# A written-out instruction order for an attention-plus-MLP kernel: another order for the last groups, four whole-array groups in place of three, and another spread of the last stores

## The chip, the cores and the metric

The kernel runs on one core of a Trainium2 chip. A core has five engines that run side by side, each through its own list of instructions in order: TensorE (PE, matrix products), VectorE (DVE), ScalarE (ACT), GpSimd (POOL) and SyncE (SP, which here issues transfers). They wait for each other through semaphores. Matrix products land in eight banks of accumulator memory, which PE writes and which DVE and ACT can read. Transfers between on-chip memory and device memory (DMA) are issued from the queues of SP, ACT and POOL.

The metric is the device time of one execution in microseconds (us). The profile adds a span: the time from the first to the last instruction of one profiled execution.

## The reference

The reference has two stages. The first is attention with 32 learned "inducing" rows over each of four sequences of 12,480 tokens with 128 channels, done twice (the 32 rows attend to the tokens, then the tokens attend to the result). The second is a two-layer network with 2,048 hidden units and a PReLU on all 49,920 tokens.

```
def mab(q, kv):
    s = scale * (q @ kv.transpose(0, 2, 1))
    a = np.exp(s - s.max(-1, keepdims=True))
    a /= a.sum(-1, keepdims=True) + 1e-09
    return a @ kv
h = mab(I, x)             # 32 x 128 for each sequence
x = mab(x, h)             # 12480 x 128 for each sequence

h = x @ w_in              # 128 -> 2048
g = np.maximum(h, 0.0) + alpha * np.minimum(h, 0.0)
out = g @ w_out           # 2048 -> 128
```

## The kernel before

**The algebra.** The tokens' attention output is a weighted sum of 32 rows, so the kernel never forms it. It multiplies those 32 rows by `w_in` beforehand (`h_weights`, tile `hW`), and the hidden layer then is one product of contraction length 32: the tokens' unnormalised attention weights (tile `rep`, 32 rows, copied four times over the 128 partitions) times `hW`. PReLU is split into a linear part, done by one small matrix (`hA`, function `linear`), and a ReLU part, `relu(h)` times the scaled output weights (`W1`). The attention's denominator is divided out at the very end (`rdT`).

**Groups and chunks.** The 49,920 tokens are cut into 100 groups of up to 512 tokens, 25 for each sequence; the last group of each sequence has 192 tokens. For each group the 2,048 hidden units are 16 chunks of 128. A *fill* (function `fill`) computes one chunk into a bank: a matmul of 32 rows, on one of four row tiles of PE. Then ACT (line 750) or DVE (line 752) empties the bank with a ReLU into a tile `gt`: an *eviction*. In the 192-token groups a fill is two matmuls of 192 columns into one bank, and the eviction is 384 columns wide. A *second* (function `second`) multiplies a chunk's `gt` by `W1` and adds it to the group's own accumulator bank.

**Row tiles.** PE can work as four row tiles of 32 rows each, which run side by side. A second is therefore cut into four matmuls, one for each quarter of the chunk's 128 hidden units. Row tiles must not add to one bank at the same time, so a group goes through row tile 0 for all 16 chunks, then row tile 1, and so on: row tile 3 is the last and works on an older group than row tile 0 does. A second can also be one matmul over the whole array, all 128 rows at once. The constant `WHOLE` (line 25) says how many of the last groups are added up in that way; it was 3, groups 97, 98 and 99.

**The order.** The order of the instructions is written out by hand in the string `PLAN`. Each letter is a step of PE:

- `a` to `h` with a digit: a fill. `a b` are on row tile 0, `c d` on 1, `e f` on 2, `g h` on 3. The first of each pair is emptied by ACT, the second by DVE. The digit is the bank.
- `w x y z`: the next second of row tile 0, 1, 2, 3.
- `v`: the next second over the whole array.
- `l` and `m` with a digit: a group gets its accumulator bank, and the linear part is added (`m` for the groups of `WHOLE`).
- `s` with digits: a pause, in which the products for the attention of a later stretch run.

`pin` ties every instruction to the one recorded before it on the same engine, so the order of the calls is the order on each engine. A fill must wait until its bank has been emptied, a second until its `gt` has been written, and an eviction until its fill is done.

**The end of a group.** After a group's last second, `finish` runs: DVE transposes the accumulator (line 818, `ot`), POOL multiplies by the reciprocal denominators (line 826, `ob`), and four transfers store the result (line 851). `to_end` counts the groups still to come. Until the last four groups all stores are issued by POOL. For the last ones the table `queues` names other queues, and for the last two DVE does the multiplication in whole or in half.

Of the kernel before, what the change touches and what calls it, by code (L numbers as in the profile page):

```python
# [16 lines left out]
P = 128  # L17
# [7 lines left out]
WHOLE = 3  # L25
# [175 lines left out]
b02h12c223a312s4h212b012a323c12313f413s23e01h112l2wg42d33w231w3e03w32d1w31we431w3f31w3e01w32w3d1  # L201
2w3c42w32wd3g02w132w12h1wc4232xa02h3xa523x23b4x23a1x23xl0w23wxxwf3g5xw3e4s1h5xe3wxe4w3xwf13xw23x
wxe3wh5x2w32wc43wyd13wyc6wg3ys5b4yya1d6ywya5yyg3xb43xy3ya1xyxh6yc53yxh3ya4x3xy3xb1xza6zl5xe7zwxf
3zwc4wzwf1zxwe6zwh7xwzc3wzxwg4d1wzxwe6xzwf7zwzc3ywywzd4ywzc1yzl6yxwg7yxg3wxywh4xywxya1xywxyh2a7x
ywxyb3xya4xywd1ywxe2wxzf7s342zf1xwzxwe3zxwf7zwc2zwyc4zwyd1zwyzyc3zyxb7zyxg2yxb4zyxza1yxzyxb3ze7x
zyxl2yxwg4yxwyxwg1yxwh3yxwxg7wf4xzwxe0zwze1wzywd3zywzyc7wzyd4wzyc0wzwf1zwyza3yza7xyzb4xyza0xzyxl
1zyxwyxwg3yxwh7xywg4yxwh0xywg5xwzxe3wxzwf7xzwxze4wxf5zwc0zwzd3yws745d0wzywyzc3b7yzyzxa4yzxl5yzxb
0yzxa3yzxwzxywxg7ywxg4ywyxh0wyg3xwyxwyxh7wxe6wxzf4wxze0wxze3wzwd7zywc6zywzywd4zyc0zyxb3zyxzya7xz
yb6xzya4xzyl0xzywxg3ywxzywxg7ywxyh6wxywg4xe3wxzwxf2zwxzwe7xzwe4d6zwyzwyd3zwyzc2wyzd7wyza6yzl4xyz
wxyg3b2xyzxwyza6xyzb7xyzwxyg3wxyg2wxyh6ywxwxwxe7zs312xzb7e6xzwf3xzwe2xzwzwc1zywd6yzwc7yzwd2yzwza  # L210
3yzyb1xyzxa6zyxl7zyxwh2yxa3yxzwyxwg6yxwg1yxwyxwh3yxwg2xwe6xwzf5xwzxwze1xwzf3c2wzwzywd6yzwc5yzyzd
1yzb3xyzxa2yzxa6yxzl5yxzwyxza1yxzwyxg2wyxh3wyxg6wyxwyxh1wxe0wxze2wxzwxf3zwze6wzywzyc0wzyd1wzywc2
zyd3l6zyxwzya0xzyb1xzywxzya2zxyzxwys3012xh4ywxg3ywxywh0xywg2xe1wxwzf4xwzxwe3zxwzf2xwzc0wzd1wyzwy
c4zyza3yzxb2yzxl0yzxwyzc1b4yzxwyzxa3yzxwyg2xwyxwh1yxg4wyxwyxg3wyd7wxwe2zxwf1zxwzxwe4zxwf3zc7wzc2
ywzyd1zyxzya4xzb3yxza7yxzyxb2zyxzl1yxg4wyxwh3yxwg7yxzwyxzwyc2ywxg4yxwf3xwze7xwzxwf2s5437wyzd2wyz
c5wyzwyzd4we3zwyzb7yza2yzxya5zxyb4zxyl3zxywxzf7a2xzywxzywxg5ywxg4ywxyh2wxg7wxwxzf5wxze6wxze4wxzw
zd2wzywzc7ywzd6ywzyc5za4yzb2xyzxyl7zxywzxyb6g5xywzxywzxya4xywg2xywh6xywxywg5xwf4xwze0xwzf2xwze6x
wzwzd5ywzc4ywzc0ywzyl6zd2wzyxwzyxzya4xzyb5xzya0xzywxg2ywxzywxywh4xywg5xywxyg0wxs2154wxe0zwxf2zwx
e1zxwze4d5zwzywd0zywc2zyl1yzxwyzxa5zyxb4zyxwyzc2b0yzxwyzxa5yxwzyxwg4yxwg2yxwh0yxwyxwg5xwf4xzwe3x
zwxzwf2c0zwzd5ywyzwyzc4l3yzwxzya2xzyb0xzywxe5zwd4yzwxzya2xzywxzya0xywxh5ywxg4ywxywxg2ywxh0wxe7zw  # L220
xf4zwxzwe5c2zwyzwd0yzl7ywzxya4xzf5wzxywyzc2b0yzxwyzxa4yzxb5yzxwzyc2wzyxs0452ywxg0f6wxg4ywxg5ywxh
2ywxs0d6we4zxwzxwze5xwzf2c0wzd4zyl6yxzwxyza5xyzb2xyzwc0yzwxyzb4xyza5xyzwxyza2xyzwxywg0xyh4wxyg5x
wys21045wxywxh2e1wxf4zwc5zwyzwyc0zwyd1zwyc2zyzb5xyza4xyzl0xyzwxyza1xf2zwxzywxf4g5wxyzwxyza1xzywx
yg2wxyg5wxyh4wxwxf1zwxe3zwzwc2yzwyd5wzyc4wzyzl3d1yzwxyza2xyzwxf5zwxe4zwxyzb1xyza2xywzxyzwc5ywxyg
4wxyg1b2xywxywxe5b7xzwe4xzwd2zwxe1zwd5zwyc7zwyzc4yb2zxyl1zxywzxya5h7yxwzyxwg4d2ywzywxza5yxzyb7xz
xywg4ywxzywxg2yxwe5wxf7wzxf4xzws2657wxzf2wzc4wzyd6wzyc7l5zywwzxywwwzxe2b4zxywwzxywa7h6xywwxzywwx
zwe2wb4xyzwxwzya7xzyl6xywxg2ywxyh4wxywg7xywxwf0c2zwyxzxwxyxh4wc7yzxwyxzxwxe2d0zwyxzxwyxzwc7f4zxw
yxzxwyc2zb0yxzxxyza7xyzb4xyzxya2zxyzl0xywg7xywxyh4ywyxe2zwxyzwyxyyh3we7xzwyxyzywyxe4h2wxyzwyxyyz
wyc7f3zwyzwyc4zwyd2zwyzwc7yzyb3zxya4zxyzxa2yzxl7yzxzwyzzxa3zf4zxzwzyzxzwzyg2xywh1xwyzxg3wyxzzwxz
ze4wzxf2wzxwe1zxwzf3c5wzywzyc4wzyd2wzyc1zwyb3zyza5xyzxyb4zxya2zxyl1xzywxze3xwyh5xwyg4xwyxwyg2xwy  # L230
h3s6452xzwf3xzwe6xzwe4xzwf2xzwc5zwzwyd3wzywd6zywc4zya2zyl5zyxwh3yxwzyxwg4yxb6zyxwzyxa2yzxwyxwyg3
xwyxh4ya6xwe2xwxzf0wxzwxe3zwxzf6wzc4wzywd2zywc0zyzya3zxb6yzxyl4zxywzc2b0yzxywzxya3zxywg6xywxyh2w
xywg0xyg3wxywh7xwe6xzwxzwf2xzwe0xzwd3zwyzc7wyzwyza6d2yzl0xyzwxyg3wd7yzwxyzwxe6zb2xyzwxyza3xyzwxy
a7xywh6xyg2wxywxyg3wxf1wxwzxe7wzxf2zwc6zwyzwd3yzc1yzxa7yzxb2yzxl6yzxwyzc3b1yzxwyzxwyg7xb2yzxwyzx
we3zwxyg1wxywxywxh7ys23517xwzf2xwze3xwzf7c5wzwzyc1wzyd2wzya3zyzyxb7zyxa5zyxb1zyxl2zyxwze3xwzyd7w
yxg5wyxzwyxg1wyxg3wyxh7wyxwxg5wxzf1wxze4wxzwzd3wzyc7wzyd5wzyc1l4zyxwzyxa3zf7xwzyxwze1xzb5yxzwyxz
# [12 lines left out]
s6352zxya7zxyb6zxyl5zc3ywzd2ywzxya7zxywxzyb6xg3ywxzywxze2wxzywxyg7wxywc3h6ywxf2wxzwe0xzwxze7wzd6
wyzwyc3zb0yza2xyzxya7zxyb6zxyl3zxywzc0ywh2xywzxywg7d6ywzxywzxe0wzxywg2xywxywxh7e6wxe0zwxzwxf1zwc  # L250
2zwyzwd6yza7yzl0xyg1wxh2ywxzya6xh7wyxzwyc1zwyxh2wyxg6wyxzwyd7zwyc1zwyxzwf2xg6wyxzwyxzwe7xwf1zxwz
xe6l2wzxwwzxwwwzc7ywb4zxwwzyxa6yzxb1yzxwwyzxa7s4617xyzb6xyza4xyzwb7xzywa1xyzwxyzwwxl6yg4xwyxwyg7
xwyh1xwywxyg4xxwf5zwyzxc7wyzwyd1zwyzc4wyxzxwxe5zd7wyzxwyxzxwe1zxxwf4zxxxyza5yxzl7yxzwyc1zwyxzwyx
g4wyxh5wyxwyxg1wyyxzwyyxg3ywf4zxwzxywye5zxb1yzxwyyzxe3wzxwf4zxwyyyzc5wyyzyl1zyc3wzyxwzyxb4zyc5wz
yxwzyxa3zyxwzzyzxwzg4yd5wzyxwzzzyxwg3yd0wzzyzxwzg4yxwzyxwzzg5xwf3xzwe0xzwxzl4f2xzwe5xzwzxyb3zxya
0zxywzxyb2zc5ywxywzd3ya0zyxwzyxwzyc2wh5yxwzywxg0ywc3zywxyg2wxywxwxg5f0wxzxzf6ze3xzxyl2zxya0zxyb5
zxyzwxyza6xyzwxywzc3ywzd0ya5zxywzxywzxe6wzxys3056h7xywg3xywh0xywyxwg6f5wwzyc7wzywzyc3wzyd6a0zyzy
xb7zxya5zxyb3zxyl6zxywze0xwzxywze7d5wzxywze3xwzxywxg0ywxh7ywxyg5wxwf3xzwe1xzwe0zwyzd7wc5yzwyzd1y
zxa3yzxyzb0xyza7xl5yzxyzwd1g3wyxzwyxzf0a7xzywxzywxg1ywxh3wyxwyg7xwxe0wzxf1zwxe4wzwzyc7wyd3zwyzwc
0yzd1yl4zxywzxyza7xf3zwxyza0xywh1xywzxya7zxyb3zxywg0xywxzywxg1ywxe7wxzf3wxzwxe0zwf1zwyzc2wyzd7wy  # L260
# [47 lines left out]
def kernel(  # L308
# [9 lines left out]
    nc = tc.nc  # L318
# [490 lines left out]
    def finish(st, g, acc):  # L809
        pp, nb, _ = shape_of(g)  # L810
        t = pp * nb
# [38 lines left out]
        for a, queue in enumerate(queues):  # L850
            pin(queue.dma_start(  # L851
                out=dst[a],
# [271 lines left out]
```

## Time and profile before

| what | value |
|---|---|
| time, median of 3 runs | 543.78 us (542.15 to 545.15) |
| span of the profiled execution (its own time: the page gives the span alone) | 540.4 us |
| PE busy | 526.3 us (97%) |
| DVE busy | 504.2 us (93%) |
| ACT busy | 496.3 us (92%) |
| POOL busy | 394.7 us (73%) |
| evictions by ACT and by DVE | 906 and 662 |

The page shows one execution. "Busy" counts the time in which an engine had an instruction at work. Instructions of one engine overlap (two evictions that follow each other start less than one duration apart), so a busy share near 100% does not say that nothing more would fit. A row of a group gives the source line, the engine, the operation, output and input, the count, and then the busy time, the mean duration in ns and the idle time of the engine ahead of these instructions with what ended most of it. A row in order of time begins with its start and its duration in us; `xN` says that N like instructions are merged, and the duration then runs from the first start to the last end. `32*128 32x512` is a matmul on 32 rows and 128 columns of the array with 512 columns streamed; in a merged row the shape of the first one is shown.

### The profile page before, as it was taken

To read this page: it belongs to the slowest core of one execution; us is meant where nothing else is said; L and a number is where in the kernel's file an instruction comes from. 1 tells how busy PE (TensorE), PEld (TensorE's weight loads), DVE (VectorE), ACT (ScalarE), POOL (GpSimd) and SP (SyncE) were. 2 spreads that over 40 slices of the span, in tenths; PEclk is the share of its full clock that TensorE was granted. 3 is DMA by queue.
4 is the path that set the end of the run, shared out by engine and by line. 5 is a ranking of instruction groups with operands and counts; after the bars stand their busy time and mean duration, and the time that the engine had idled before them with its cause. 6 is when DMAs were issued, how large, how long until landed. Compare 5 with 4: busy or idle time off the path is not lost.

```text
span 540.4 us, 21603 instructions
## 1 busy us (share of the span) xinstructions
PE 526.3 (97%) x8988; PEld 332.7 (62%) x8988; DVE 504.2 (93%) x865; ACT 496.3 (92%) x994; POOL 394.7 (73%) x574
## 2 busy tenths in 40 slices
PE   4999999999999999999999999999999999999996
PEld 4655566566567566666667666666666566666653
DVE  3699999999989999999998999999999999999994
ACT  2499999999989999999999999999999999999950
POOL 5553778687667987687687987776767876776764
PEclk9999999999999999999999999999999999999998
DMA  8999999987799898887799797864354344334324
GB/s 197 212 186 139 182 185 156 170 142 113 112 175 149 134 160 152 162 129 145 117 153 166 117 164 158 168 101 113 66 93 113 66 96 112 70 89 108 68 42 85
DMA packets 114738, 71.12 MB, mean 132 GB/s; under 512 B 86784, under 2 KB 102784, under 8 KB 114640
## 3 DMA queue, kind: packets, MB, share of 16 engines
q0 software_dynamic: 19456, 38.62, 38.9%
q1 hardware_dynamic: 91984, 30.22, 32.9%
q8 instruction: 70, 1.15, 0.9%
q10 hardware_dynamic: 3200, 0.90, 0.7%
q14 instruction: 28, 0.23, 0.2%
HBM read 41.00 MB, written 28.95 MB: 129 GB/s over the span
## 4 chain that ended last, share of the span: by engine, by line
PE 90%; DMA 4%; DVE 2%; ACT 1%; POOL 1%; issue 1%; SPq 0%; POOLq 0%; DVEq 0%
PE bank L383 90%; DMA xn<-in_x_dram 2%; DMA rep<-e2d 1%; ACT gt L750 1%; DVE gt L752 1%; DMA e2d<-e 1%; POOL xn L412 0%; DVE ot L818 0%; PE bank L458 0%; ACT e L656 0%; DVE xT L461 0%; POOL ob L826 0%; DVE fr L608 0%; SPq L671 0%; POOL out_dram L851 0%
## 5 line engine op out<-in xcount | busy, mean ns | idle before, releaser
L383 PE MATMUL bank<-gt,W 32*128 32x512 bf16 (+1 forms) x6256 | 480.3, 371 | 0.1
L750 ACT ACTIVATE gt<-bank 128x512 bf16<-128x512 f32 (+1 forms) x906 | 464.5, 612 | 6.9 <-PE bank L383 4.6
L752 DVE TENSOR_SCALAR gt<-bank 128x512 bf16<-128x512 f32 (+1 forms) x662 | 417.7, 677 | 9.9 <-PE bank L383 6.1
L383 PE MATMUL bank<-rep,hW 32*128 32x512 bf16 (+1 forms) x1600 | 418.4, 368 | 1.5 <-DMA rep<-e2d 1.3
L383 PEld LDWEIGHTS <-W 32*128 32x128 bf16 x6256 | 264.4, 92 | 146.5 <-issue 46.6
L851 POOL DMA_DIRECT2D out_dram<-ob x386 | 247.3, 669 | 37.7 <-POOL ob L826 30.4
L826 POOL TENSOR_TENSOR ob<-ot,rdT 128x512 f32<-128x512 f32 (+2 forms) x99 | 106.3, 1074 | 93.8 <-DVE ot L818 79.5
L383 PEld LDWEIGHTS <-hW 32*128 32x128 bf16 x1600 | 136.9, 92 | 20.8 <-issue 5.1
L818 DVE STREAM_TRANSPOSE ot<-bank 128x512 f32<-128x512 f32 (+1 forms) x100 | 69.9, 699 | 6.7 <-PE bank L383 5.6
L383 PE MATMUL bank<-rep,hA 32*128 32x512 bf16 (+1 forms) x100 | 36.1, 367 | 0.0
L427 POOL DMA_DIRECT2D xn<-in_x_dram x32 | 20.7, 663 | 0.1
L481 ACT ACTIVATE e1t<-bank 128x256 bf16<-128x256 f32 (+2 forms) x14 | 5.0, 356 | 10.8 <-PE bank L383 10.8
L461 DVE COPY xT<-bank 128x1024 bf16<-128x1024 bf16 (+1 forms) x13 | 8.5, 650 | 4.9 <-PE bank L458 4.4
L383 PE MATMUL bank<-xT 32*128 32x512 bf16 x81 | 12.5, 376 | 0.0
L553 ACT ACTIVATE e<-bank 128x512 bf16<-128x512 f32 x18 | 11.0, 610 | 0.2 <-PE bank L383 0.2
L656 ACT ACTIVATE e<-bank 128x512 bf16<-128x512 f32 x18 | 11.1, 614 | 0.1
L383 PEld LDWEIGHTS <-xT 128*128 128x128 bf16 (+1 forms) x177 | 8.0, 97 | 4.1 <-issue 1.5
L383 PEld LDWEIGHTS <-hT 128*32 128x32 bf16 (+1 forms) x122 | 3.6, 93 | 11.0 <-issue 10.9
L383 PE MATMUL bank<-xT,hT 128*32 128x512 bf16 (+1 forms) x98 | 10.3, 388 | 0.0
L383 PEld LDWEIGHTS <-hA 32*128 32x128 bf16 x100 | 9.2, 92 | 1.8 <-issue 0.6
L458 PE MATMUL bank<-ident,xn 128*128 128x128 bf16 x96 | 9.0, 249 | 1.0 <-DVE xn L963 0.9
L412 POOL DMA_DIRECT2D xn<-in_x_dram x11 | 6.2, 583 | 3.3 <-DMA xn<-in_x_dram 2.5
(87 smaller groups left out, 131.7 us busy)
## 6 DMA issues: line engine op xcount, KB each, us to landing
out_dram<-ob POOLq DMA_DIRECT2D x373, 64.0 KB, 3.2
rep<-e2d SPq DMA_DIRECT2D x92, 128.0 KB, 3.2
xn<-in_x_dram POOLq DMA_DIRECT2D x37, 256.0 KB, 5.5
e2d<-e SPq DMA_DIRECT2D x24, 128.0 KB, 3.6
xn<-in_x_dram POOLq DMA_DIRECT2D x4, 512.0 KB, 8.2
rdT<-rt SPq DMA_DIRECT2D x96, 8.0 KB, 2.6
early<-in_moe_w_out_dram POOLq DMA_DIRECT2D x4, 256.0 KB, 10.6
xT<-xn SPq DMA_TRANSPOSE x36, 5.2
```

The lines of the kernel that those rows point to most:

```text
L383: return pin(nc.tensor.matmul(o, lhsT, rhs, start=start, stop=stop, **kw))
L412: pin(nc.gpsimd.dma_start(out=xn[:, q0:q1, :], in_=src[:, q0:q1, :]))
L427: pin(nc.gpsimd.dma_start(out=st.xn[u][:, part, :], in_=src[:, part, :]))
L458: pin(nc.tensor.transpose(tp[:, k * P : (k + 1) * P], xn[:, q, j * C : (j + 1) * C], ident[:]))
L461: pin(nc.vector.tensor_copy(out=st.xT[:, u, qs[0] : qs[-1] + 1, :].rearrange("c q t -> c (q t)"), in_=tp[:, : len(qs) * GRP],))
L553: pin(nc.scalar.activation(out=e1[:], in_=ps[:], func=EXP, scale=scale, accum_out=st.es[:, u : u + 1]))
L656: pin(nc.scalar.activation(out=e2[:].rearrange("p (t j i) -> p t j i", j=n, i=32), in_=turned(ps[:pp, :w], n), func=EXP, scale=scale_of(st ...
L750: pin(nc.scalar.activation(out=gt[:, :w], in_=ps[:, :w], func=RELU))
L752: pin(nc.vector.tensor_relu(gt[:, :w], ps[:, :w]))
L818: pin(nc.vector.transpose(out=ot[:, :t], in_=acc[:, :t]))
L826: pin(engine.tensor_tensor(out=ob[:, k0 * w : k1 * w].rearrange("p (k m c) -> p k m c", k=k1 - k0, c=32), in0=ot[:, k0 * w : k1 * w].rearr ...
L851: pin(queue.dma_start(out=dst[a], in_=ob[32 * a : 32 * a + 32, :t].rearrange("p (b k) -> p b k", k=32),))
```

## The change

The plan is replaced. Its letters are the same in the same order up to a place in group 94, some 35 us ahead of the last matmul; in that part only the digits of banks differ here and there (another of the free banks is named). From there on the order is new. `WHOLE` goes from 3 to 4: group 96, too, is added up over the whole array. Its sixteen `v` come in small runs between the steps of the row tiles, and so do those of groups 97 and 98.

The last stores are now named in a table: `S` is SP, `A` is ACT, `P` is POOL. Its first entry is for the group that finishes last, the second for the one before it, and so on for five groups. In the order in which they finish, the last five groups were 95, 97, 98, 96 and 99, and are now 94, 97, 95, 98 and 99. For the last but one, DVE's half of the multiplication and the four stores are held back until the last group's own stores have been issued.

```
-WHOLE = 3
+WHOLE = 4
+LAST_STORES = ("SASA", "PPAS", "SASA", "PSPS", "SSSS")
...
 PLAN = """
...
-1zwyc2zwyd5zwyd7zya4zxya1zxyzxyb2zxyg5xyzd4yg7xyzxyh1xya2zxyxyg5xyh4xe7xzxf2zxe1zxzc5e6zyzb7yzyb
-4zc1yzyzyh5yh2yb6zyd7zyzyzyh1ym4zyb5zvvvvvvvvvvvvvvvvyd2m6h7yh1d5vvvvvvvvvvvvvvvvzzd3m4zzzzzf2zz
-zzb7f1b5zzzzzvvvvvvvvvvvvvvvv
+h4vzyf6wwc3zwyzc1yvb4yzzxzyxc3e6vvvb1zzxyyxyxg3vb4zzxxyyc6zxzzyyxye3vb1xxzzxxg6e4vvs3vb0xzxzxg6e1vvv
+c3yzyzh4yg6yvvvd0zze1ym3ze4vvvd6yyzzyyg7b1zvvvc0a4zyzyyb7h6vvvvva1yzzyyyc0g7h4vvvvc6zzzf1za2vm0zg4zv
+vd7za1zzf6ze2vvva3zzze4d1vvvve7zc2a6zzb3d1vvvvvvvm4g7g5f2vvvvvvvvvvvvvvvv
 """
...
+    held = []
...
     def finish(st, g, acc):
...
-        if to_end == 0:
-            scaled(nc.vector, 0, nb)
-        elif to_end == 1:
-            scaled(nc.gpsimd, 0, nb // 2)
-            scaled(nc.vector, nb // 2, nb)
-        else:
-            scaled(nc.gpsimd, 0, nb)
...
-        queues = {
-            3: (nc.sync,) * 4, 2: (nc.scalar,) * 4,
-            1: (nc.sync, nc.scalar, nc.gpsimd, nc.sync),
-            0: (nc.scalar, nc.gpsimd, nc.scalar, nc.sync),
-        }.get(to_end, (nc.gpsimd,) * 4)
-        for a, queue in enumerate(queues):
-            pin(queue.dma_start(...))
+        def store():
+            by = LAST_STORES[to_end] if to_end < len(LAST_STORES) else "PPPP"
+            for a, name in enumerate(by):
+                queue = {"P": nc.gpsimd, "S": nc.sync, "A": nc.scalar}[name]
+                pin(queue.dma_start(...))
+
+        def second_half():
+            scaled(nc.vector, nb // 2, nb)
+            store()
+
+        if to_end == 0:
+            scaled(nc.vector, 0, nb)
+            store()
+            for fn in held:
+                fn()
+        elif to_end == 1:
+            scaled(nc.gpsimd, 0, nb // 2)
+            held.append(second_half)
+        else:
+            scaled(nc.gpsimd, 0, nb)
+            store()
```

More of the change, by code (lines that the diff above doesn't have):

```diff
@@ new lines @@
+wxe2wxzf1s754zf2xwzxwe1zxwf7zwc4zwyc5zwyd2zwyzyc1zyxb7zyxg4yxb5zyxza2yxzyxb1ze7xzyxl4yxwg5yxwyxwg2yx
+wh1yxwxg7wf5xzwxe0zwze2wzywd1zywzyc7wzyd5wzyc0wzwf1zwyza2yza7xyzb5xyza0xzyxl1zyxwyxwg2yxwh5xywg7yxwh
+0xywg6xwzxe2wxzwf5xzwxze7wxf0zwc6zwzd5yws270d6wzywyzc5b7yzyzxa2yzxl0yzxb6yzxa5yzxwzxywxg7ywxg2ywyxh6
+wyg5xwyxwyxh3wxe7wxzf2wxze6wxze5wzwd3zywc7zywzywd2zyc6zyxb3zyxzya5xzyb7xzya2xzyl6xzywxg3ywxzywxg5ywx
+yh7wxywg2xe3wxzwxf4zwxzwe5xzwe7d2zwyzwyd3zwyzc4wyzd5wyza2yzl7xyzwxyg3b4xyzxwyza5xyzb2xyzwxyg3wxyg4wx
@@ L304 @@
+zzwc5wzyyd3zyzyxa1zb7xya4yxzxyl5zzxwa3yzwxh1wyxyxg7wwg4xwzzyyyxyxxs31g7wyxwxyxwf4xwd3g6zwe1wwyyyzzm7
+h4vzyf6wwc3zwyzc1yvb4yzzxzyxc3e6vvvb1zzxyyxyxg3vb4zzxxyyc6zxzzyyxye3vb1xxzzxxg6e4vvs3vb0xzxzxg6e1vvv
+c3yzyzh4yg6yvvvd0zze1ym3ze4vvvd6yyzzyyg7b1zvvvc0a4zyzyyb7h6vvvvva1yzzyyyc0g7h4vvvvc6zzzf1za2vm0zg4zv
+vd7za1zzf6ze2vvva3zzze4d1vvvve7zc2a6zzb3d1vvvvvvvm4g7g5f2vvvvvvvvvvvvvvvv
 """
@@ L844, in finish @@
             dst = out[t0 : t0 + REM, :].rearrange("(i b) (a k) -> a i b k", b=t // 32, k=32)
-        queues = {
-            3: (nc.sync,) * 4, 2: (nc.scalar,) * 4,
-            1: (nc.sync, nc.scalar, nc.gpsimd, nc.sync),
-            0: (nc.scalar, nc.gpsimd, nc.scalar, nc.sync),
-        }.get(to_end, (nc.gpsimd,) * 4)
-        for a, queue in enumerate(queues):
-            pin(queue.dma_start(
-                out=dst[a],
-                in_=ob[32 * a : 32 * a + 32, :t].rearrange("p (b k) -> p b k", k=32),
-            ))
+        def store():
+            by = LAST_STORES[to_end] if to_end < len(LAST_STORES) else "PPPP"
+            for a, name in enumerate(by):
+                queue = {"P": nc.gpsimd, "S": nc.sync, "A": nc.scalar}[name]
+                pin(queue.dma_start(
+                    out=dst[a],
+                    in_=ob[32 * a : 32 * a + 32, :t].rearrange("p (b k) -> p b k", k=32),
+                ))
+        def second_half():
[12 more added lines that the diff above has]
+            store()
         st.rep.pop(g)
```

189 lines of the change are left out of this document (89 added, 100 removed).

## The prediction

> **What bounds the kernel now.** I read the page first (busy time, slices, the chain that ended last), then stretches of the last 40 us, then single instructions of that stretch in order of time. The page:
>
> ```profile
> span 540.4 us, 21603 instructions
> PE 526.3 (97%) x8988; PEld 332.7 (62%) x8988; DVE 504.2 (93%) x865; ACT 496.3 (92%) x994; POOL 394.7 (73%) x574
> PE 90%; DMA 4%; DVE 2%; ACT 1%; POOL 1%; issue 1%; SPq 0%; POOLq 0%; DVEq 0%
> L750 ACT ACTIVATE gt<-bank 128x512 bf16<-128x512 f32 (+1 forms) x906 | 464.5, 612 | 6.9 <-PE bank L383 4.6
> L752 DVE TENSOR_SCALAR gt<-bank 128x512 bf16<-128x512 f32 (+1 forms) x662 | 417.7, 677 | 9.9 <-PE bank L383 6.1
> ```
>
> PE carries 90% of the chain; ACT and DVE, which empty the banks, are nearly as full. That holds until the tail, where ACT runs dry and the clock falls (columns: the stretch, then busy us per engine or PE alone, the granted clock):
>
> ```profile
> 500.50:520.30 19.80, 19.48 (x39) 1.00 0.31 61
> 520.30:535.75 15.45, 0.00 (x0) 0.89 0.38 69
> ...
> 528.75:532.15 3.40, 3.40 (x28) 1.00 0.32 58
> 532.20:535.55 3.35, 3.35 (x19) 0.50 0.70 117
> ```
>
> The first pair is ACT's evictions (L750): none after 520.3. The second is PE: after a stretch in which it was busy but mostly with one row tile, the clock is halved, and the last group's matmuls run in that half-clock stretch. So the tail is set by PE, and within PE by row tile 3 (`z`), which still has a whole group to add up alone at 529-532. Its steps:
>
> ```profile
> 529.53 0.59 PE L383 MATMUL bank<-gt,W 32*128 32x512 bf16 x2
> ...
> 521.13 3.72 PE L383 MATMUL bank<-gt,W 32*128 32x512 bf16 x16
> 524.47 0.59 PE L383 MATMUL bank<-gt,W 128*128 128x512 bf16 x2
> 525.00 0.39 PE L383 MATMUL bank<-rep,hA 32*128 32x512 bf16 x1
> ...
> 506.88 0.37 PE L383 MATMUL bank<-rep,hW 32*128 32x512 bf16 x1
> 507.18 0.26 PE L383 MATMUL bank<-xTr,hT 128*32 128x192 bf16 x1
> ...
> 532.49 3.27 PE L383 MATMUL bank<-gt,W 32*128 32x512 bf16 x17
> ```
>
> Two matmuls of one row tile last 0.59 together and 0.37 each, so they start 0.22 apart; I use 0.216. Whole-array matmuls (`v`) keep that step but occupy all four row tiles: the second row merges the last `z` of group 95 with fifteen `v`, whose sixteen starts lie within 3.35 (one change of 0.3, then fourteen steps of 0.217). A change between row tiles and another tiling of the array is dearer: 506.88 to 507.18 is 0.30 into it; out of it, the second `v` of the 524.47 row starts at 524.68 and the next row at 525.00, 0.32. So a change costs 0.09 over a step. The last row holds the end of `z` and the sixteen 192-column `v` of the last group, 0.16 apart at half clock; the last starts at 535.42.
>
> **The change, part by part.**
>
> *Work per row tile.* From the first letter whose kind differs (in group 94) to the end, row tile 3 has 152 jobs in both plans, of which 48 and 64 are `v`: turning group 96 from 64 row-tile steps into 16 `v` removes nothing from `z`. What differs is how often the four row tiles must meet. A run of `v` starts when all four are done, so each stretch between runs costs its longest row tile. Counted from the two plans: before, 29 + 20 + 40 + 2 + 16 = 107 steps and 32 long `v`, 139; after, 94.6 steps over 19 stretches and 48 long `v`, 142.6. The difference, 3.6 x 0.216 = +0.8 us.
>
> *Changes of tiling.* Before: 3 runs of `v` and two pauses, 9 changes. After: 19 runs (of 1 to 7, the last of 16) and the same pauses, 39. 30 x 0.09 = +2.7 us. Nothing hides them: every row tile stands still in them. Bounds: 0.07 to 0.11 each, +2.1 to +3.3.
>
> *The clock.* After, the longest stretch of `z` alone is four steps, and `v` fills the array between; I take the full clock to the end. Then the last group's `v` step is set by the weight load:
>
> ```profile
> L383 PEld LDWEIGHTS <-e 128*128 128x128 bf16 x4 | 0.2, 96 | 0.1
> ```
>
> 0.10 instead of 0.16, sixteen times: -1.0; and the two slow steps of the 532.49 row (0.37 from 532.12, and 0.56 to the first `v`, against 0.22 and 0.31) go: -0.4. Bounds 0 (half clock again) to -1.4; I take -1.4. PE's last start without a new wait: 535.4 + 0.8 + 2.7 - 1.4 = 537.5.
>
> *A wait that is added on ACT.* In the new table group 95's stores go SASA. Two of them are on ACT's queue, and in the instruction order they stand **ahead of the last two evictions of group 99** (the fills `g7 g5`). In the kernel before, ACT's stores came after its last eviction, so nothing was queued behind them. Now ACT waits there for POOL's multiply of group 95, issues twice, and only then empties two banks that `v` 10 to 13 of group 99 need. The rows for the chain:
>
> ```profile
> 525.17 0.72 DVE L818 STREAM_TRANSPOSE ot<-bank 128x512 f32<-128x512 f32 x1 [0.71 <-PE bank L383]
> ...
> 523.77 0.69 DVE L818 STREAM_TRANSPOSE ot<-bank 128x512 f32<-128x512 f32 x1
> 524.54 1.07 POOL L826 TENSOR_TENSOR ob<-ot,rdT 128x512 f32<-128x512 f32 x1 [2.64 <-DVE ot L818]
> ...
> 530.06 1.07 POOL L826 TENSOR_TENSOR ob<-ot,rdT 128x512 f32<-128x512 f32 x1 [0.48 <-DVE ot L818]
> 531.16 1.51 ACTq L851 DMA_DIRECT2D out_dram<-ob  x2
> ...
> 500.71 1.09 ACT L750 ACTIVATE gt<-bank 128x512 bf16<-128x512 f32 x2
> ```
>
> From the start of group 95's last `z`: 0.49 to the transpose (524.68 to 525.17), 0.72 for it, 0.08 to POOL, 1.07 there, 0.03 to the issue (531.13 to 531.16), 1.51 for two: 3.9. Evictions of 512 start 0.49 apart on ACT (1.09 for two of 0.60); for 384 columns I take 0.4 and 0.5: the second bank is empty at 4.85, with the signal 4.9. PE from the same start: 0.31 to the next `v`, seven of them to 1.6, 0.31 out, about 0.5 for the last fills and the way back in: the first `v` of group 99 at 2.4, the thirteenth at 2.4 + 12 x 0.10 = 3.6. It waits 1.3 us. Bounds: 0.6 (half clock, `v` arriving later) to 1.7; I take +1.3. PE's last start: 538.8, 3.4 later than before.
>
> *The end behind PE.* Rows of before:
>
> ```profile
> 535.86 0.38 DVE L818 STREAM_TRANSPOSE ot<-bank 128x192 f32<-128x192 f32 x1 [1.46 <-PE bank L383]
> 536.28 0.36 DVE L826 TENSOR_TENSOR ob<-ot,rdT 128x192 f32<-128x192 f32 x1
> 536.66 0.57 SPq L851 DMA_DIRECT2D out_dram<-ob  x1
> 536.67 1.49 ACTq L851 DMA_DIRECT2D out_dram<-ob  x2
> 536.94 0.54 POOL L851 DMA_DIRECT2D out_dram<-ob  x1 [0.44 <-DVE ob L826]
> 537.29 0.87 ACTq L851 DMA_DIRECT2D out_dram<-ob  x1
> 533.97 0.42 DVE L826 TENSOR_TENSOR ob<-ot,rdT 128x256 f32<-128x256 f32 x1
> ```
>
> The last issue starts at 537.29, and the span ends 3.1 later. After, group 99's four stores take two issues on SP and two on ACT, and the half of group 98 that was held back (0.42 on DVE) and its four stores follow: a third issue on ACT starts after 1.49, at 538.2 on the old scale, not 537.29; POOL's two start behind the held half, near 537.1 and 537.8. DVE's last multiply also waits for 15 signals instead of 7, of which the transpose covers some: 0 to 0.35, taken as 0.1. Together +1.0, bounds +0.4 to +1.3. The holding itself spares the last DVE eviction 0.42, which nothing was late for.
>
> *What costs nothing.* Eleven evictions go from DVE to ACT (906 to 917): 11 x 0.49 = 5.4 us, inside ACT's 15.45 idle us; without that cover it would be added in full. The stores of groups 94 and 97 move to SP and POOL, whose next work is other stores. Up to the tail every engine has the same order; 199 of about 1500 hand-overs of a bank name another bank. DVE's whole wait for PE is 6.1 us; 13% of it, 0.8, up or down, taken as 0.
>
> Sum: 0.8 + 2.7 - 1.4 + 1.3 + 1.0 = **+4.4 us**. The profiled span goes from 540.4 to 544.8. The median of the runs is 543.78, 3.4 above the span; the same step on it gives **548.2 us**, 0.8% slower. A difference of 0.5%, 2.7 us, is about what a measurement of this kernel can tell from none (its three runs lie within 3.0).
>
> **The rivals.**
>
> *A, the wait and the changes are partly covered.* If POOL's multiply and ACT's issues come earlier than I count (wait 0), the issues at the end cost +0.4, and bank names give -0.8: 0.8 + 2.7 - 1.4 + 0.4 - 0.8 = +1.7, 545.5: not to be told from no change. For it: the pairs of fill and first use are 2 to 5 us apart over most of the new tail. Against it: the ACT order above is fixed. 0.21.
>
> *B, matmuls of different row tiles start strictly in the program's order.* The new plan has far more neighbours on one row tile (`z z`, `y y`, `www`); were each matmul to wait for the start of the one ahead, I count 24 steps more after and 2 more before: 22 x 0.216 = +4.7 on top, 552.9. The trace speaks against it. The old plan has `z z d3 m4 z` behind group 98's last `v`:
>
> ```profile
> 529.09 0.25 PE L383 MATMUL bank<-rep,hW 32*128 32x192 bf16 x1
> 529.10 0.25 PE L383 MATMUL bank<-rep,hA 32*128 32x192 bf16 x1
> 529.31 0.37 PE L383 MATMUL bank<-gt,W 32*128 32x512 bf16 x1
> ```
>
> `d3` and `m4` (the first two) start 0.2 before the second `z`, which stands ahead of them. So order binds only through a full queue: 0.07. The Trainium skill, TensorE: Matmul & The Clock Gate, in Part 3 (the mechanism), states the rule of this rival: matmuls start and end in program order, and only weight loads are pulled ahead. By that rule the sum would be +9.1; the rows disagree with it.
>
> *C, faster.* The other bank names let PE refill sooner during the first 500 us. It decides from 4.4 us (even) and 7.1 us (0.5% faster). For it: many hand-overs are tight, and DVE and ACT wait 6.1 and 4.6 us for PE. Against: only 13% are changed, and 7.1 would be two thirds of all that waiting. 0.07; at 7.1 it gives 541.1.
>
> **How the numbers follow.** My forecast 0.65, A 0.21, B 0.07, C 0.07. Slower by over 0.5%: forecast and B, 0.72; within: A, 0.21; faster: C. The forecast's own bounds: low ends 0.8 + 2.1 - 1.4 + 0.6 + 0.4 - 0.8 = +1.7, high ends 0.8 + 3.3 - 0 + 1.3 + 1.3 + 0.8 = +7.5. The range runs from 544.6 (half way into A, +0.8) to 551.3 (+7.5), leaving C, part of A and most of B outside.
>
> **What would show it.** PE's granted clock stays 1.00 to the end of PE. The last 40 us hold some 39 starts about 0.31 behind their neighbour, against 9. ACT shows two store issues ahead of its last two evictions, with an idle gap put down to POOL's `ob`, and PE stands for over 1 us inside the last run of `v`. PE's last start comes 3.4 later, and the span ends 6.0 behind it instead of 5.0. Up to 500 us both traces keep the same pace. I am wrong if that pace differs by more than 1 us, if the change of tiling is cheaper in short runs, or if PE waits for evictions elsewhere in the new tail.

## The result, and the profile after

The changed kernel takes 549.9 us (median of 4 runs, 549.05 to 551.4); the kernel before, in runs beside it, 543.5. The ratio is 1.0121, 95% interval 1.0089 to 1.0154: slower by 6.4 us. The profiled execution took 550.31 us with a span of 548.5.

The page of the changed kernel (the line numbers have moved by four):

```profile
span 548.5 us, 21513 instructions
PE 529.0 (96%) x8936; PEld 330.4 (60%) x8940; DVE 499.6 (91%) x854; ACT 503.3 (92%) x1005; POOL 393.3 (72%) x572
PE 89%; DMA 4%; POOL 1%; issue 1%; ACT 1%; DVE 1%; SPq 1%; POOLq 0%; ACTq 0%; DVEq 0%
L746 ACT ACTIVATE gt<-bank 128x512 bf16<-128x512 f32 (+1 forms) x917 | 471.4, 609 | 19.5 <-PE bank L379 13.1
L379 PE MATMUL bank<-gt,W 32*128 32x512 bf16 (+1 forms) x6204 | 481.9, 371 | 1.7 <-ACT gt L746 1.2
L748 DVE TENSOR_SCALAR gt<-bank 128x512 bf16<-128x512 f32 (+1 forms) x651 | 412.8, 679 | 17.9 <-PE bank L379 13.4
```

PE is still the chain. New is the end of its row: 1.2 us in which PE itself waits for ACT. The two engines that empty the banks wait for PE more than before (13.4 and 13.1 us, against 6.1 and 4.6): idle time of theirs that costs nothing, and that shows PE has fallen behind them.

The 8.1 us between the two spans fall into three stretches. A is the start, in the same execution, of the same matmul in both plans (one of the last two fills ahead of the place in group 94 where the order differs), B the start of the last matmul, C the end of the span:

```
                      before    after    difference   forecast
A  common place       500.02    501.39     +1.37        0
A to B  new tail       35.40     39.36     +3.96       +3.4
B to C  behind PE       4.96      7.77     +2.81       +1.0
```

Spans and medians differ because executions scatter: the one profiled of before is near the low end of its runs (A below shows where the scatter sits).

The tail on PE, in order of time (start, duration from the first start to the last end):

```profile
512.89 0.37 PE L379 MATMUL bank<-rep,hW 32*128 32x512 bf16 x1
513.20 0.82 PE L379 MATMUL bank<-gt,W 128*128 128x512 bf16 x3
513.96 0.38 PE L379 MATMUL bank<-rep,hW 32*128 32x512 bf16 x1
...
537.54 0.50 PE L379 MATMUL bank<-rep,hW 32*128 32x192 bf16 x6
537.97 1.00 PE L379 MATMUL bank<-gt,W 128*128 128x192 bf16 x10
540.12 0.87 PE L379 MATMUL bank<-gt,W 128*128 128x192 bf16 x6 [1.16 <-ACT gt L746]
```

The first three rows are one short run of `v`: in at 0.31, three starts 0.22 apart, out at 0.32. All 37 such changes that the trace has after 500 us (before: 7) look like it, apart from a few beside short matmuls and two of 0.53, where a row tile had one step more to do. The last two rows are the last run: ten `v` 0.083 apart, a stop of 1.2 us, six more.

ACT, DVE and POOL over the same end, and two rows of the waits (us in total, times, longest):

```profile
538.00 1.54 ACTq L840 DMA_DIRECT2D out_dram<-ob  x2
539.58 0.87 ACT L746 ACTIVATE gt<-bank 128x384 bf16<-128x384 f32 x2 [2.75 <-POOL ob L823]
542.22 2.19 ACTq L840 DMA_DIRECT2D out_dram<-ob  x3
...
541.11 0.38 DVE L815 STREAM_TRANSPOSE ot<-bank 128x192 f32<-128x192 f32 x1 [2.23 <-PE bank L379]
541.83 0.73 DVE L823 TENSOR_TENSOR ob<-ot,rdT 128x192 f32<-128x192 f32 x2 [0.34 <-DVE ot L815]
...
536.89 1.08 POOL L823 TENSOR_TENSOR ob<-ot,rdT 128x512 f32<-128x512 f32 x1 [2.81 <-DVE ot L815]
538.51 0.63 POOL L823 TENSOR_TENSOR ob<-ot,rdT 128x256 f32<-128x256 f32 x1 [0.54 <-DMA rdT<-rt]
543.17 1.29 POOL L840 DMA_DIRECT2D out_dram<-ob  x2 [4.03 <-DVE ob L823]
```

```profile
POOL out_dram L840 <- DVE ob L823: 4.0, 1, 4.0
ACT gt L746 <- POOL ob L823: 2.7, 1, 2.7
PE bank L379 <- ACT gt L746: 1.2, 1, 1.2
```

The chain inside the tail reads from POOL upwards: POOL multiplies group 95 until 537.97, ACT issues that group's two stores from 538.00 to 539.54, empties its last two banks from 539.58, and PE goes on at 540.12. The chain behind PE: transpose to 541.49, 0.34 of waiting for signals, DVE's two multiplies to 542.56, POOL's two stores only from 543.17. Then the program closes on two engines side by side. SP's closing block waits for the last landing (the row below, of SP's own queue): by the profile that is ACT's third store, landed at 546.78, with POOL's second store landed before it, at 546.41. SP is through its block at 547.36. POOL's own closing instruction, a drain, ends at 547.73 and is the last.

```profile
SPq L1124 <- DMA out_dram<-ob: 2.5, 1, 2.5
```

The clock held in the changed kernel (stretches: from and to, length, busy us of PE, granted clock):

```profile
531.50:534.90 3.40, 3.24 (x22) 1.00 0.65 112
534.90:538.30 3.40, 3.40 (x33) 1.00 0.22 33
538.30:541.20 2.90, 1.49 (x15) 1.00 0.55 90
```

### The profile page after: what moved, and what is told of

It reads as the page before. It is cut to its first block, busy times and chain, and to the rows that moved or that the text cites. A ratio compares the mean times of both kernels' runs of the same rounds, so it can differ in the third digit from the quotient of the medians.

```text
span 548.5 us, 21513 instructions
## 1 busy us (share of the span) xinstructions
PE 529.0 (96%) x8936; PEld 330.4 (60%) x8940; DVE 499.6 (91%) x854; ACT 503.3 (92%) x1005; POOL 393.3 (72%) x572
## 4 chain that ended last, share of the span: by engine, by line
PE 89%; DMA 4%; POOL 1%; issue 1%; ACT 1%; DVE 1%; SPq 1%; POOLq 0%; ACTq 0%; DVEq 0%
PE bank L379 89%; DMA xn<-in_x_dram 2%; DMA xT<-xn 2%; ACT gt L746 1%; DMA out_dram<-ob 0%; POOL xn L408 0%; POOL ob L823 0%; POOL out_dram L840 0%; SPq L667 0%; PE bank L454 0%; DVE ot L815 0%; SPq L428 0%; DVE xT L457 0%; DVE fr L604 0%; ACTq L840 0%
## 5 line engine op out<-in xcount | busy, mean ns | idle before, releaser
L746 ACT ACTIVATE gt<-bank 128x512 bf16<-128x512 f32 (+1 forms) x917 | 471.4, 609 | 19.5 <-PE bank L379 13.1
L748 DVE TENSOR_SCALAR gt<-bank 128x512 bf16<-128x512 f32 (+1 forms) x651 | 412.8, 679 | 17.9 <-PE bank L379 13.4
L379 PEld LDWEIGHTS <-W 32*128 32x128 bf16 (+1 forms) x6208 | 261.2, 92 | 147.6 <-issue 49.9
L379 PEld LDWEIGHTS <-hW 32*128 32x128 bf16 x1600 | 135.5, 92 | 25.1 <-issue 8.1
```

The lines of the kernel that those rows point to most:

```text
L379: return pin(nc.tensor.matmul(o, lhsT, rhs, start=start, stop=stop, **kw))
L746: pin(nc.scalar.activation(out=gt[:, :w], in_=ps[:, :w], func=RELU))
L748: pin(nc.vector.tensor_relu(gt[:, :w], ps[:, :w]))
```

## The experiments

The theory to be tested was the prediction's own sum with its sizes corrected: the order (changes of tiling), the ACT wait and the end behind PE each carry a part, and the names of banks carry none. Its rivals: the names cost what A shows, or one of the parts hides behind another. "Tail" below is A to B, "end" is B to C, both of the profiled execution; ratios are to the kernel before, run beside it. Rows without another word are instructions in order of time, of the kernel named ahead of them.

**The names alone, and the rest alone.** `names_alone` has the new names up to the common place, and behind it the old order (its banks renamed to match), the old stores and `WHOLE = 3`. `tail_alone` is the reverse: the new order and stores, with the old names throughout.

```diff
 PLAN = """        # names_alone: only bank digits differ from before
...
-yd2m6h7yh1d5vvvvvvvvvvvvvvvvzzd3m4zzzzzf2zzzzb7f1b5zzzzzvvvvvvvvvvvvvvvv
+yd1m2h7yh5d0vvvvvvvvvvvvvvvvzzd3m4zzzzzf1zzzzb7f5b0zzzzzvvvvvvvvvvvvvvvv
```

> The old kernel with only the other bank names up to the place in group 94 (the old tail follows, its digits renamed to fit). In the two profiles the new kernel was 1.4 us late at that place, with steps of 0.9 us near 152-158 us and 0.3 us twice before 270 us. Theory that the names cost it: the span is about 541.8 and the median 1.4 us (0.25%) above before, with the same steps at the same groups. Rival, that those steps are the difference of two executions (late transfers): 0 within 0.5 us, and the steps lie elsewhere or are absent.

> The changed kernel with the old names of the banks throughout: only the order of the last 800 places and the stores are new. Theory that the names are worth what they cost alone (ratio 1.0011, 0.9998 to 1.0023): the ratio is 1.010 to 1.012, PE reaches group 94 within 0.3 us of the kernel before apart from the step at 152 us that varies between executions, the two steps of 0.3 us at groups 41 and 45 to 47 are gone, the tail on PE is 39.4 and the end behind it 7.75. Rival, that the names carried the whole +1.37 us by which the changed kernel was late at group 94: the ratio is near 1.009. Rival, that the new tail costs less on its own than beside the new names: the tail on PE falls under 38.5.

`names_alone`: 542.57 us against 541.71, ratio 1.0011 (0.9998 to 1.0023); A +0.39, tail 35.68, end 5.01. `tail_alone`: 549.11 against 541.33, ratio 1.0143 (1.0121 to 1.0165); A -0.30, tail 39.35, end 7.78. So the loss is in the tail and the end, with either set of names. (Compared place by place, the two plans write another digit at most places of the first part, because one other choice renames what follows; the 199 hand-overs of the prediction are the places where a bank comes from another step.)

The starts of the same fills, in all kernels, show what A is made of. Up to 148 us all agree within 0.4, `act_four` within 0.6. Between 149 and 158 us, where the second sequence begins, they part by -1.7 to +1.9, with old and new names alike. At 152 us PE waits for the copy that spreads `e` over the partitions, for as long as the transfer happens to be late. In the order before, after, names alone:

```profile
152.28 0.39 PE L383 MATMUL bank<-rep,hW 32*128 32x512 bf16 x1 [1.32 <-DMA rep<-e2d]
```

```profile
152.63 0.38 PE L379 MATMUL bank<-rep,hW 32*128 32x512 bf16 x1 [1.64 <-DMA rep<-e2d]
```

```profile
151.76 0.39 PE L379 MATMUL bank<-rep,hW 32*128 32x512 bf16 x1 [0.65 <-DMA rep<-e2d]
```

In `two_parts` and `held_no_pool` below it does not wait there at all, and they are 1.7 and 1.5 us earlier at that place. The changed kernel loses 0.3 us there and 0.7 at 158 us, where PE waits for another transfer (`xT`). The latest one, `stores_alone` (+1.9), lost 1.6 of it to a stretch at half clock, from 152.6 to 156.1. All this comes and goes with the execution. What does belong to the names is smaller: two steps of 0.3 us, at groups 41 and 45 to 47, are there in every kernel with the new names and in none with the old. Some 0.25 us of these 0.6 is won back by 480 us, again in every kernel with the new names, so that 0.3 us is left, which neither ratio resolves from nothing.

**The mark again.** The changed kernel, unaltered, in more rounds.

> The changed kernel itself, timed in more rounds, as the mark from which the partly undone kernels are counted. If the new names cost nothing that shows, the ratio is that of the kernel with the old names and the new tail, 1.0143 (1.0121 to 1.0165), within the intervals: 1.012 to 1.015. If the new names cost 0.1% or more on top of the tail, it is 1.015 or higher. If the old names were the dearer ones, it stays under 1.0125. PE reaches group 94 somewhere from -1.5 to +1.9 us against the kernel before, with the two steps of 0.3 us at groups 41 and 45 to 47; the tail on PE is 39.4, the end behind it 7.75.

549.11 us against 542.18, ratio 1.0113 (1.0074 to 1.0152). It lies on both sides of the bounds that I had set (under 1.0125 by its median, up to 1.015 by its interval), so the cost of the names stays unresolved below some 0.3%. A is +2.23, of which 1.7 came at one place, another late transfer in this execution:

```profile
406.62 0.39 PE L379 MATMUL bank<-rep,hW 32*128 32x512 bf16 x1 [1.48 <-DMA rep<-e2d]
```

Tail 39.36 and end 7.75 are those of the first profile to 0.02 us. These two are therefore what the following kernels are judged by, beside the ratio. The ratios alone would not do: the intervals of the kernels in which one part is undone overlap that of the changed kernel, so the size of a part is read from one trace of each.

**The ACT wait.** Group 95's stores leave ACT's queue, or all four go onto it:

```diff
-LAST_STORES = ("SASA", "PPAS", "SASA", "PSPS", "SSSS")
+LAST_STORES = ("SASA", "PPAS", "SSSS", "PSPS", "SSSS")   # no_act_store
+LAST_STORES = ("SASA", "PPAS", "AAAA", "PSPS", "SSSS")   # act_four
```

> The new kernel with group 95's stores all on SP, so that nothing stands ahead of ACT's last two evictions. Theory of the added wait: the pause of 1.2 us inside the last run of v and the 0.2 us after it go, the last start of PE comes 1.4 us earlier, and the median falls by 1.4 us (549.9 to 548.5). Rival, that the last run would then wait for the next late thing (DVE's eviction, or SP's longer queue at the end): less than 0.5 us gained.

> The new kernel with all four stores of group 95 on ACT: the suspected wait is doubled. Two issues took 1.54 us, so the last two evictions of ACT come 1.5 us later, the pause inside the last run of v grows from 1.2 to 2.7 us, and from the place in group 94 to PE's last start it takes 40.8 us instead of 39.4. If the pause has another cause, it stays.

`no_act_store`: 547.33 us, ratio 1.0106 (1.0086 to 1.0125); tail 37.82, 1.54 shorter; end unchanged at 7.76. ACT now empties the banks at once, and the last run has no stop:

```profile
536.35 0.87 ACT L746 ACTIVATE gt<-bank 128x384 bf16<-128x384 f32 x2 [1.07 <-PE bank L379]
...
536.41 1.49 PE L379 MATMUL bank<-gt,W 128*128 128x192 bf16 x16
```

`act_four`: one run, 551.88 us; tail 40.72, 1.36 longer. ACT and PE:

```profile
538.04 2.72 ACTq L840 DMA_DIRECT2D out_dram<-ob  x4
540.80 0.87 ACT L746 ACTIVATE gt<-bank 128x384 bf16<-128x384 f32 x2 [3.92 <-DMA out_dram<-ob]
...
541.35 1.18 PE L379 MATMUL bank<-gt,W 128*128 128x192 bf16 x6 [2.34 <-ACT gt L746]
```

Two stores more, 1.2 us more on ACT's queue, 1.2 us more of waiting on PE (1.16 to 2.34, where 2.7 was expected). The other 0.2 of the 1.36 is the clock: it is halved from 540.9 on in this execution, and the last `v` start up to 0.16 apart. The mechanism is shown from both sides.

**The changes of tiling.** Seven runs of `v` are put together with the run behind them, 19 to 12 runs; the steps are the same ones, and the longest row tile has one less to go through.

```diff
-h4vzyf6wwc3zwyzc1yvb4yzzxzyxc3e6vvvb1zzxyyxyxg3vb4zzxxyyc6zxzzyyxye3vb1xxzzxxg6e4vvs3vb0xzxzxg6e1vvv
+h4zyf6wwc3zwyzc1yvvb4yzzxzyxc3e6vvvb1zzxyyxyxg3b4zzxxyyc6zxzzyyxye3vvb1xxzzxxg6e4vvs3vb0xzxzxg6e1c3y
...
```

> The new kernel with seven of the nineteen runs of v moved on into the next one (12 runs, 14 changes of tiling fewer, 1 slot less on the longest row tile). Theory of the price per change, 0.095 each: 14 x 0.095 + 0.2 = 1.5 us earlier at PE's last start, if the wait on ACT moves along with it; the median falls by 1.5. Rival, that the changes lie in time in which PE would wait anyway for evictions: under 0.4 us gained, and waits for gt appear in front of the longer runs.

546.75 us, ratio 1.0092 (1.0074 to 1.0109); 25 changes instead of 37, tail 37.51, 1.85 shorter. That is more than the runs alone give, and the profile shows why:

```profile
534.42 1.54 ACTq L840 DMA_DIRECT2D out_dram<-ob  x2
536.06 0.87 ACT L746 ACTIVATE gt<-bank 128x384 bf16<-128x384 f32 x2 [2.40 <-PE bank L379]
...
535.35 0.50 PE L379 MATMUL bank<-rep,hW 32*128 32x192 bf16 x6
535.78 1.70 PE L379 MATMUL bank<-gt,W 128*128 128x192 bf16 x16
```

With `v` moved back, group 95 ends earlier, and ACT's two stores begin 0.93 us ahead of the last fills (535.35) instead of 0.47 behind them (538.00 against 537.53). The last run takes 1.70 from its first start to its last end; in `no_act_store` it takes 1.49, in the changed kernel 3.02 (537.97 to 540.99). So 1.3 of the 1.85 is ACT's wait, and some 0.5 is what is left for twelve changes: 0.045 each net, where the starts alone say 0.095. And these 0.5 hold two more things: the one step less (0.2 by the expectation), and a wait of 0.20 for an eviction of DVE's in front of one of the longer runs (532.62), as the rival had it, though small. The run does not separate these parts well: it shows the direction of the changes' price, not its size.

**The end behind PE.** `not_held` multiplies and stores group 98 at once, with its store on ACT moved to SP; `held_no_pool` keeps the held half, but POOL stores none of it.

```diff
-LAST_STORES = ("SASA", "PPAS", "SASA", "PSPS", "SSSS")
+LAST_STORES = ("SASA", "PPSS", "SASA", "PSPS", "SSSS")   # not_held
-            held.append(second_half)
+            second_half()
...
+LAST_STORES = ("SASA", "SASA", "SASA", "PSPS", "SSSS")   # held_no_pool, held as it was
```

> The new kernel with the second half of group 98 multiplied and stored at once instead of being held back; its stores go to POOL twice and SP twice, none to ACT. Theory that the stores behind the last multiply set the end: from the last start of PE to the end of the span 7.75 us becomes 5.4 (only two stores on SP and two on ACT are left, and DVE still waits for a long list of signals), the median falls by 2.0 to 2.4 us. Rival, that the end is set by what closes the program on POOL whatever is stored last: less than 0.7 us gained. PE's last start unchanged within 0.5.

> The changed kernel with the second last group's held half kept, but its four stores on SP, ACT, SP, ACT instead of POOL, POOL, ACT, SP, so POOL stores nothing at the end. The end behind PE's last start is 7.75 us in the changed kernel and 5.07 with neither hold nor POOL stores so late. Theory that POOL's store carries a part of it (its first store starts 0.56 us behind the held half and its drain ends 3.9 us after the second one starts, where an SP or ACT store is landed some 2.2 us after its start): the last issue on ACT starts near 2.2 us behind the last group's first, so the end behind PE is 6.6 to 6.9 us, ratio to the kernel before some 0.002 under the changed kernel's, near 1.010. Theory that the hold alone carries it (the four stores of 64 KB come last in the queues whichever engine issues them): end stays at 7.5 to 7.8 and the ratio at 1.011 to 1.012. PE's tail stays at 39.4 in both.

`not_held`: 546.32 us, ratio 1.0084 (1.0062 to 1.0105); tail 39.37, end 5.07, 2.70 shorter and within 0.1 that of the kernel before. POOL's stores are issued before PE starts its last matmul (539.77):

```profile
538.72 1.29 POOL L840 DMA_DIRECT2D out_dram<-ob  x2 [0.30 <-POOL ob L823]
...
540.64 0.36 DVE L823 TENSOR_TENSOR ob<-ot,rdT 128x192 f32<-128x192 f32 x1
541.03 1.50 ACTq L840 DMA_DIRECT2D out_dram<-ob  x2
```

`held_no_pool`: 547.59 us, ratio 1.0114 (1.0094 to 1.0134); tail 39.37, end 7.25:

```profile
539.44 0.73 DVE L823 TENSOR_TENSOR ob<-ot,rdT 128x192 f32<-128x192 f32 x2 [0.34 <-DVE ot L815]
539.83 2.57 SPq L840 DMA_DIRECT2D out_dram<-ob  x4
539.83 2.88 ACTq L840 DMA_DIRECT2D out_dram<-ob  x4
```

Neither theory had the number: taking the stores off POOL gives back 0.5 of the 2.7 us, the other 2.2 stay with the holding. The 0.5 is a net figure. POOL's drain no longer ends last, but four issues now stand on each of two queues, and the last, of 64 KB, starts 3.7 us behind PE's last start (542.05): 3.1 behind it in the changed kernel, 1.9 in the kernel before.

**The new stores on the old order.** `LAST_STORES` and the holding, with the plan and `WHOLE` of before.

```diff
-WHOLE = 4        # of the changed kernel
+WHOLE = 3
...              # and the plan of the kernel before
```

> The old plan and three whole-array groups, with the new table of the last stores and the held half. Theory that the order of the last stores costs by itself: from PE's last start to the end of the span 5.0 us becomes 7.7, the median rises by 2.7 (0.5%). PE's last start stays within 0.5, because in the old plan ACT has no eviction left behind its stores. Rival, that it hurts only together with the new plan: 0 within 0.7.

542.93 us against 541.56, ratio 1.0031 (1.0013 to 1.0049): slower, by 1.4 to 1.7 us, half of what I expected. The end is the expected 7.72. The tail was 34.63 in the profile, 0.77 under before, because the half clock came later in that execution (stretches of that kernel, columns as above):

```profile
531.00:534.90 3.90, 3.90 (x33) 1.00 0.55 96
534.90:537.00 2.10, 1.98 (x14) 0.51 0.42 69
```

That accounts for 0.8 us of the profile; whether it happens in most executions, I did not try.

**Three parts undone together.** The edits of `no_act_store`, `not_held` and `fewer_runs` in one kernel.

> The new kernel with all three edits at once: no store on ACT for group 95, nothing held back, twelve runs of v in place of nineteen. If the three prices add up (1.5, 2.7 and 1.85 in the profiles), the span is 6 us shorter than the new kernel's and the median lies within 1 us of before (0 to +0.2%). If two of them hide behind each other, it stays 1.5 us or more above before (over +0.3%).

544.79 us against 541.56, ratio 1.0061 (1.0039 to 1.0083), not the 1.002 at most that I expected. Tail 37.61, end 5.98. The end is 0.9 longer than in `not_held`: group 95's four stores, now on SP, are still ahead of the later ones there, and SP's last issue starts 2.2 us behind PE's last start and is landed 2.5 later (1.9 and 1.9 in `not_held`). The ACT edit adds nothing to `fewer_runs`, which had already moved the stores out of the way; and DVE is next in line:

```profile
537.33 0.42 DVE L823 TENSOR_TENSOR ob<-ot,rdT 128x256 f32<-128x256 f32 x1
537.68 0.55 DVE L748 TENSOR_SCALAR gt<-bank 128x384 bf16<-128x384 f32 x1
538.71 0.38 DVE L815 STREAM_TRANSPOSE ot<-bank 128x192 f32<-128x192 f32 x1 [0.49 <-PE bank L379]
```

The half that is no longer held (537.33) stands ahead of DVE's last eviction (537.68 to 538.23), and PE starts its last two `v` at 538.28: this is what the holding was worth, 0.3 us. Three of this execution's changes took 0.53 instead of 0.31. The parts are thus not a sum that can be taken off one by one.

**What of the new order could help the old one.** The prediction counted 1.4 us for the full clock. `two_parts` is the kernel before with its sixteen `v` of group 98 cut in two and the `z` of group 96 put on both sides, so that `z` never stands alone for long. `two_parts_queues` adds other queues for the last stores.

```diff
-yd2m6h7yh1d5vvvvvvvvvvvvvvvvzzd3m4zzzzzf2zzzzb7f1b5zzzzzvvvvvvvvvvvvvvvv
+yd2m6h7yh1d5vvvvvvvvzzd3zzzzzf2zvvvvvvvvm4zzzb7f1b5zzzzzvvvvvvvvvvvvvvvv
...
-            3: (nc.sync,) * 4, 2: (nc.scalar,) * 4,          # two_parts_queues
-            1: (nc.sync, nc.scalar, nc.gpsimd, nc.sync),
-            0: (nc.scalar, nc.gpsimd, nc.scalar, nc.sync),
+            3: (nc.sync,) * 4, 2: (nc.sync, nc.scalar) * 2,
+            1: (nc.sync, nc.scalar) * 2,
+            0: (nc.gpsimd, nc.sync, nc.gpsimd, nc.scalar),
```

> The old kernel with group 98's sixteen v cut in two runs of eight, and the sixteen steps of row tile 3 cut in two likewise, so that row tile 3 never works alone for a whole 3.4 us window: two more changes of tiling (+0.2). Theory that the half clock of the old tail came from that lone stretch: the clock stays full until PE ends, the last sixteen v go from 0.16 to 0.083 apart, PE ends 1.2 to 1.4 us earlier, net -1.1 (-0.2%). Rival, that any window in which row tile 3 works alone for half the time still halves the clock: +0.2.

> The kernel before with the two long runs cut into 8 + 8 as in two_parts, and with the stores of the last three groups put on other queues: the third last on SP and ACT in turn (before: all four on ACT), the second last on SP and ACT in turn, and of the last group two small stores on POOL, one on SP, one on ACT. In two_parts PE's last start came 1.3 us earlier and the end behind it grew by 1.5 us, to 6.46: ACT was still issuing the third last group's stores when the second last group's were ready, and POOL's drain ended 3.1 us after its last store. Theory that the queue of stores is what ate the gain: end behind PE 5.1 to 5.5, tail on PE still 34.1, so 1.0 to 1.3 us under the kernel before in the tail, ratio 0.998 (0.997 to 0.999). Rival, that the two last groups simply finish too close together (their transposes and multiplies on DVE and POOL, 1.2 us apart instead of 2.6): end behind PE stays at 6.2 to 6.5 and the ratio is 1.000 to 1.001.

`two_parts`: 541.74 us against 541.56, ratio 1.0011 (0.9993 to 1.0030). The clock is full to the end of PE, and the tail is 34.08, 1.3 shorter (stretches, columns as above):

```profile
526.40:529.80 3.40, 3.35 (x25) 1.00 0.31 58
529.80:533.20 3.40, 2.86 (x25) 1.00 0.44 77
```

But the end grew from 4.96 to 6.46. `two_parts_queues`: 541.56 against 541.33, ratio 1.0000 (0.9989 to 1.0012); tail 34.07, end 6.09. The queues give back 0.4, and its profile shows the rest:

```profile
533.54 0.43 DVE L822 TENSOR_TENSOR ob<-ot,rdT 128x256 f32<-128x256 f32 x1
533.58 0.87 POOL L822 TENSOR_TENSOR ob<-ot,rdT 128x256 f32<-128x256 f32 x1 [1.01 <-DVE ot L814]
533.95 0.38 DVE L814 STREAM_TRANSPOSE ot<-bank 128x192 f32<-128x192 f32 x1
534.37 0.36 DVE L822 TENSOR_TENSOR ob<-ot,rdT 128x192 f32<-128x192 f32 x1
535.69 1.13 POOL L847 DMA_DIRECT2D out_dram<-ob  x2 [1.24 <-DVE ob L822]
```

The two last groups are ready for their stores at 534.45 and 534.73, all eight stores at once. In the kernel before, the half clock kept them 1.8 us apart (POOL's half ready at 534.89, DVE's last multiply at 536.64), and the first group's stores went out beside PE. So the rival of that run held, in its ratio and nearly in its end (6.09, under its 6.2): taking the half clock away gained the kernel before nothing that can be measured. That this is because the stores, all ready at once, wait for one another is argued from these rows, not tested by itself. No kernel here beats the one before by what can be measured.

## Why the prediction was right, and where its sizes were off

The direction came out as forecast, and the time inside the range: 549.9 us against 548.2, slower by over 0.5%. The step itself was put too small, +4.4 against +6.4 between the medians and +6.8 in the tail and the end of the two traces; most of the difference is one term, the end behind PE. The steps:

- *Changes of tiling, +2.7.* 37 against 7 in the trace (39 against 9 forecast, the two pauses included), 0.31 or 0.32 from start to start where a step is 0.216: 30 x 0.095 = +2.85 by the starts. That each change stands there at that price is shown by the rows. That taking twelve away gives 12 x 0.095 is not: `fewer_runs` gave some 0.5 beside the ACT wait.
- *The clock, -1.4.* Right in size: 1.00 to the end of PE. The reason given for the new step was not: `v` start 0.083 apart, less than the mean weight load of 0.096 that was to set it. `two_parts` has the same effect alone: -1.3, with two changes more.
- *Work per row tile, +0.8.* Not measured by itself. What is left of the tail is 3.96 - 2.85 + 1.4 - 1.54 = +1.0, in which the two changes of 0.53 are 0.4.
- *The ACT wait, +1.3.* Right in place, cause and size (its addends give 4.8 for the second bank, not 4.85, which is nothing here): the row says 1.16, taking it away 1.54, with a shorter stop behind the second bank; two stores more cost +1.36.
- *The end behind PE, +1.0.* **The mis-sized term: it measured +2.8, of which `not_held` took back 2.70.** Two of its steps failed. The signals were "0 to 0.35, taken as 0.1": DVE goes through them in seven entries 0.098 apart, the transpose covered the first half, and 0.34 passed behind it. And a third issue on ACT 0.9 later was carried over with the old 3.1 us behind it. Measured, the last issues start 3.1 behind PE's last start (POOL 543.80, ACT 543.82), 1.2 later than before, and the span ends 4.7 behind them, 1.6 later than before. Of these 1.6, 0.8 is the landing: ACT's last store, of 64 KB, takes 2.96 from its start, the last one of before, of 24 KB, 2.18. The other 0.8 lies between that landing and the last closing instruction, POOL's drain (0.96, against 0.15 before, where SP's block was last). Without POOL's stores, in `held_no_pool`, the last issue starts at 542.05 and the span ends 3.6 behind it.
- *Names, 0 within 0.8.* Right as far as ratios show; 0.3 by the steps that recur. That A differs by more than 1 us, which I had named as a sign of being wrong, is for the most part the two late transfers at 152 and 158 us (1.0 of the 1.37).

Rival A (partly covered) had the ACT wait fall away and the end cost 0.4; neither did. Rival C (faster by the names) did not happen. Rival B would have made the tail 8.1 longer, not 3.96. The Trainium skill, TensorE: Matmul & The Clock Gate, Part 3, from which B's rule came, thus differs from this case's traces both in rows and in time.

## What to carry to other kernels

Shortening the work of the engine that bounds a kernel need not pay at its very end: in `two_parts` PE finished 1.3 us earlier and the stores behind it took all of it back. Read what is queued for each DMA queue when the last result is ready, before counting a gain of the last few us. A store on a compute engine's queue is an instruction like any other, and PE paid 1.2 us here for the two evictions behind it. Parts of a tail that wait for one another are not additive: test them together as well as one by one.

## What the runs showed of the hardware that was not expected

POOL's row of a store does not show when the store is done. In the changed kernel the row of POOL's second store ends at 544.46, and by the profile the store is landed at 546.41, 2.0 us later. The Trainium skill, Perfetto Trace Analysis, in DMA Instruction — SWDGE (GPSIMD), says that the recorded end of such an instruction is the end of descriptor generation, not of the transfer; these rows agree. At 2.6 us from its start the landing is no later than for a store of ACT's (the stores of 64 KB behind 537 us, with the median us from issue to landing):

```profile
out_dram<-ob ACTq DMA_DIRECT2D x3, 64.0 KB, 2.7
out_dram<-ob POOLq DMA_DIRECT2D x2, 64.0 KB, 2.5
```

What comes later is POOL's closing drain, from 543.62 to 547.73. It ends 1.32 us behind the landing of POOL's last store in all nine traces in which that store has 64 KB, and 0.42 behind it in the four with 24 KB. What the drain waits for is not shown: in `held_no_pool`, where POOL's last store was landed 2.5 us before the drain began, it still takes 3.1 us, though there it ends long before SP's block.

The clock is halved behind a stretch in which PE was busy all the time, but mostly with one row tile (3.40 of 3.40 us in the kernel before), and stays full where the same `z` alternate with whole-array `v` (`two_parts`, 3.35 of 3.40 busy). The Trainium skill, TensorE: Matmul & The Clock Gate, Part 1, speaks of idle gaps; these traces show a drop without one.
